# A transformer layer on one core: what the start of attention holds, and where its exponentials are kept

## The chip, the cores and the metric

The kernel runs on one core of a Trainium2 chip, with one launch. The metric is device time in microseconds (us) of that core. A core has a matrix engine (TensorE, "PE" in the profile, its weight loads "PEld"), a vector engine (VectorE, "DVE"), a scalar engine (ScalarE, "ACT"), GpSimd ("POOL") and a sync engine ("SP") that issues DMA transfers. Each runs its own list of instructions in order, and they wait for one another through semaphores. Data lives in SBUF (128 partitions) and in PSUM, eight banks of 128 x 512 f32 that the matmuls write.

## The reference

```python
def _A_ref(x, wqkv, wo):
    ...                                   # H = 32 heads of Dh = 32
    scores = jnp.einsum("bhqd,bhkd->bhqk", q, k) * scale
    p = _softmax(scores, axis=-1)
    o = jnp.einsum("bhqk,bhkd->bhqd", p, v)
    return (lambda x, *d: x.transpose(*d))(o, 0, 2, 1, 3).reshape(B, S, D) @ wo

def _B_ref(x, w1, b1, w2, b2):
    h = jnp.einsum("bsd,df->bsf", x, w1) + b1
    h = _gelu(h)
    return jnp.einsum("bsf,fd->bsd", h, w2) + b2

x = A_x
h = x + _A_ref(_layernorm(x, axis=-1), A_wqkv, A_wo)
h2 = h + _B_ref(_layernorm(h, axis=-1), B_w1, B_b1, B_w2, B_b2)
```

One sequence of 2048 rows, width 1024, FFN width 3584, in bf16. Nothing is masked, so every row attends to all 2048.

## The kernel before

**Tiling.** The rows are 16 tiles of 128, and eight *units* of 256 query rows (`UNITS`). The 32 heads are eight *head groups* g of four heads. A *job* (unit, g) is the attention of one unit in one head group; it has eight *rounds*, each over two key tiles, that is a chunk of 256 keys. A round is:

- a score product on PE (`Att.qk`, L787): eight matmuls into two *score units*. A score unit u is the pair of PSUM banks 2u and 2u + 1. `att.n_units` says how many there are to go round.
- two exponentials on ACT (L797), 128 x 1024 each, from the two score units into a slot of `PT`, a ring of `NR` = 8 slots.
- PV on PE (`Job.pv`, L840): eight matmuls with V into the job's PSUM bank. The denominators stand beside it in the same bank: DVE adds the halves of a slot into `PS` (L855; for units 0 and 1 it also adds two such sums, L861), and PE multiplies the sums by ones (`Job.den`, L878). Some rounds are *direct*: PE takes the exponentials themselves, eight matmuls in place of four, and DVE does nothing.
- at the end of a job `Job.finish` divides (L895 to L909) and writes a 256-wide part of `OT`, from which `wo` later makes the output projection.

PV of a round is added one or two rounds behind its score product.

**Stages.** First the *lead*. Tiles of x land in `xrb`, DVE normalises them (`layer_norm`, L588 to L607) into `xb`, PE transposes them (L613), ACT or DVE copies the result into `xnT` (L620, L622). From it PE makes Q, K and V (`proj_half` and `proj_v1` for head group 0, in chunks of two tiles; `proj` and `proj_v` for the others). In the lead, K of one chunk after the other is made for head group 0, and with each chunk hc the rounds hc of jobs (0, 0) and (1, 0) run. The score units are 0 and 1 (`att.n_units = 2`, banks 0 to 3), banks 4 and 7 serve everything else (`lead_slot`), and 5 and 6 belong to the two jobs.

After the lead the score units are 0, 1 and 2 (banks 0 to 5), and banks 6 and 7 serve all the rest (`slot`). The next jobs are those of

```python
ORDER = [(2, 0)] + [(k, g) for g in range(1, G) for k in range(2)]
```

with the projections of head group g made ahead of its jobs. Then follow units 2 to 7, each beside the FFN of units before it: `wo` (output projection, residual), `ln2`, `ffn1`, `gelu` (its tanh on ACT, L1041), `ffn2`. Queries of units 2 and up go through `q_scratch` in DRAM, made either by `proj` or, from a copy of `xnT` in `x_scratch`, by `late_q`. After the last attention job comes the *tail*: the rest of `wo`, `ln2`, `ffn1` and `ffn2` for unit 7.

`KT` and `V` hold K and V of all head groups for the whole attention. In the lead only head group 0 is in use, and `xb` lies in the area of V of groups 6 and 7.

**Order.** Nothing of the order is written by hand for each engine. Every operation is a task of a graph, with a cost (`occ`), a latency, a priority and what it reads and writes. `Graph.schedule` runs the tasks through a model of the engines, and the order in which they start there becomes each engine's order of instructions. For PE, `pick_pe` chooses: a score product first, then PV when enough rounds wait, then everything else ("bg"). The costs are those of `c_dve`, `c_act`, `MM` and so on; they are in the plan alone.

`OT` is [P, 3, G, 256]: unit qb uses part qb % 3.

Of the kernel before, what the change touches and what calls it, by code (L numbers as in the profile page):

```python
# [12 lines left out]
P = 128  # L13
# [315 lines left out]
def build_kernel(nc, A_x, A_wqkv, A_wo, B_w1, B_b1, B_w2, B_b2, out):  # L329
# [79 lines left out]
    pt_hi = top.cur  # L409
    NS = 3  # L410
    PS, B_PS = sb(top, "PS", [P, NS, 4, 256], BF, NS)
    ot_lo = Area(top.cur)
    OT, B_OT_ = sb(top, "OT", [P, 3, G, 256], BF, 3 * G, 2)
    B_OT = [B_OT_[G * i:G * i + G] for i in range(3)]
# [57 lines left out]
    B_psO = {6: B_ps[6], 5: B_ps[5]}  # L472
    B_psD = {6: gr.buf(), 5: gr.buf()}
# [9 lines left out]
    MM = 0.2195  # L483
    def c_dve_ps(n):
        return (120 + n) / 960.0 + 0.02

    def c_dve(n, x=1):
        return (62 + n / x) / 960.0 + 0.02

    def c_tt(n):  # L490
        return n / 1920.0 + 0.155

    def c_ts(n):
        return n / 3840.0 + 0.165
# [3 lines left out]
    def c_act(n, ap_bias=False):  # L498
        return 0.073 + (0.093 if ap_bias else 0.0) + n / 1200.0

    def pe(fns, occ, reads=(), writes=(), kind="bg", mode="full", prio=0, after=()):
        return gr.add(E.PE, fns, occ, 0.16, reads, writes, prio, kind, mode, after)
# [3 lines left out]

    lead_slots = []

    def lead_slot():
        s = Slot(gr.buf(), 1, (4, 7))  # L510
        s.buf.over.append(B_ps[4])
        B_ps[4].over.append(s.buf)
        lead_slots.append(s)
        return s
# [16 lines left out]
    def mm(bank, lhsT, rhs, start, stop, reads, narrow, cols=(0, 512), after=()):  # L531

        c0, c1 = cols
        occ = MM * (c1 - c0) / 512.0 + 0.003
# [14 lines left out]
    def act(fn, n, reads=(), writes=(), prio=0, ap_bias=False, kind="", after=()):  # L549
        return gr.add(E.Activation, fn, c_act(n, ap_bias), 0.14, reads, writes, prio, kind, after=after)  # L550

    def dve(fn, occ, reads=(), writes=(), prio=0):
        return gr.add(E.DVE, fn, occ, 0.08, reads, writes, prio)
# [25 lines left out]
    def layer_norm(tiles, prio, norm="dve", quick=False):  # L579
# [6 lines left out]
        for k, (x_ap, B_x, o_ap, B_o) in enumerate(tiles):  # L586
            for c in range(2):
                dve(lambda v, c=c, k=k, x_ap=x_ap: v.bn_stats(st_l[:, i + k, 6 * c:6 * c + 6], x_ap[:, 512 * c:512 * c + 512]),  # L588
                    0.68, reads=B_x if isinstance(B_x, list) else [B_x], writes=[B_stl[i + k]], prio=prio)
            dve(lambda v, k=k: v.bn_aggr(mv_l[:, i + k, :], st_l[:, i + k, :]), 0.2,  # L590
                reads=[B_stl[i + k]], writes=[B_mv[i + k]], prio=prio)
        sl = slice(i, i + n)
        if quick:
            dve(lambda v: v.tensor_copy(mvb[:, sl, :], mv_l[:, sl, :]), 0.17, reads=B_mv[sl], writes=B_mvb[sl], prio=prio)
            dve(lambda v: v.tensor_scalar(tb[:, sl, :], mvb[:, sl, 1:2], EPS_BF, None, ALU.add), 0.17,
# [5 lines left out]
        dve(lambda v: v.tensor_copy(mvr[:, sl, :], mvb[:, sl, 0:1]), 0.17, reads=B_mvb[sl], writes=B_mvr[sl], prio=prio)  # L601
        pool(lambda g: g.tensor_tensor(denb[:, sl, 0], tb[:, sl, 0], cexp[:, 0:n], ALU.pow), 0.42 + 0.157 * n,
             reads=B_tb[sl] + [B_cexp], writes=B_denb[sl], prio=prio)
        dve(lambda v: v.reciprocal(rden[:, sl, 0], denb[:, sl, 0]), 0.19, reads=B_denb[sl], writes=B_rden[sl], prio=prio)
        for k, (x_ap, B_x, o_ap, B_o) in enumerate(tiles):
            eng, cost = (dve, 0.58) if norm == "dve" else (pool, 3.8)
# [4 lines left out]
    def transposes(src_ap, B_src, bank, dst_ap, B_dst, evac, prio):  # L611
        for dc in range(DC):
            t = pe(lambda p, dc=dc: p.transpose(psb[:, bi(bank), dc * P:(dc + 1) * P], src_ap[:, dc * P:(dc + 1) * P], ident[:]),  # L613
                   0.064, reads=[B_src, B_ident], writes=[bb(bank)], prio=prio)
# [6 lines left out]
        else:  # L621
            t = dve(lambda v: v.tensor_copy(dst_ap, src()), 0.70, reads=[bb(bank)], writes=[B_dst])  # L622
# [17 lines left out]
    def ln_tiles(tts, prio, norm):  # L640
        layer_norm([x_slot(tt) + (xb[:, tt % NXB, :], B_xb[tt % NXB]) for tt in tts], prio, norm)

    def tr_tile(tt, bank, evac, prio=0):
        tc, t4 = divmod(tt, 4)
        transposes(xb[:, tt % NXB, :], B_xb[tt % NXB], bank, xnT[:, tc, :, t4 * P:(t4 + 1) * P], B_xnTt[tc][t4], evac, prio)

    def proj(which, g, tc, bank, evac, direct=False):
# [7 lines left out]
        elif direct:  # L655
            n = q_slot(0, g, 2)
            q_slots[1, g] = n + 1
# [23 lines left out]
    def load_q(qb, g):  # L681
        if qb < 2:
# [48 lines left out]
    def proj_v1(tt, g, n, bank, evac):  # L731

        for k in range(n):
            tc, t4 = divmod(tt + k, 4)
            for dc in range(DC):
# [5 lines left out]
                reads=[bb(bank)], writes=wr)  # L741
        drop(t, bank)

    def proj_half(which, hc, bank, evac):
# [13 lines left out]
        else:  # L758
            t = dve(lambda v: v.tensor_copy(dst, psum[:, bi(bank), 0:256]), c_dve_ps(256), reads=[bb(bank)], writes=wr)
# [3 lines left out]
    class Att:  # L763
# [8 lines left out]
        def qk(self, job, r):  # L772
# [575 lines left out]
```

## Time and profile before

| | us |
|---|---|
| median of 3 runs | 1092.72 (1091.21 to 1094.55) |
| the profiled execution | 1093.21 |
| its span | 1091.4 |
| PE busy | 1047.8 |
| ACT busy | 1019.5 |
| DVE busy | 789.4 |
| 1024 exponentials (L797) on ACT | 954.0 |
| 12 copies of transposed rows (L620) on ACT in the lead | 11.9 |
| 49 tanhs (L1041) on ACT | 57.9 |

The mean granted TensorE clock was 0.997 of full speed. In the profile's lines "idle before" is the time in which the engine had nothing running ahead of an instruction, and the name behind the arrow is what ended it. Matmuls overlap one another, and the profile models their ends, so a matmul's mean time is longer than the spacing of a row of them; busy PE time is the union of these, and a PE that is busy all the time isn't at its peak. ACT's busy time is a union too: an exponential is listed with a mean of 1168 ns, and 1024 of them cover 954.0 us.

### The profile page before, as it was taken

The numbers are of one execution on the slowest core, as the hardware profiler recorded it, in microseconds if no ns is written. First come the engines' busy times: TensorE is split into PE (matmuls) and PEld (weight loads), VectorE is DVE, ScalarE is ACT, GpSimd is POOL, SyncE is SP. The second block draws the span as 40 slices with busy tenths as digits, with TensorE's granted clock in tenths as the row PEclk, the third lists the DMA queues.
The fourth block names the chain that finished last, engine by engine and source line by source line (L and its number), as shares of the span: only waits on it lengthen the run. The fifth ranks groups of instructions, "written<-read, shape, count | busy, mean of one in ns | idle before, by whom it ended". The sixth has DMA issues, their size and how long they took to land.

```text
span 1091.4 us, 41529 instructions
## 1 busy us (share of the span) xinstructions
PE 1047.8 (96%) x18880; PEld 610.0 (56%) x18930; DVE 789.4 (72%) x1518; ACT 1019.5 (93%) x1124; POOL 28.2 (3%) x78
## 2 busy tenths in 40 slices
PE   7999999998999999999999999999999999999998
PEld 5655555553457446644565466447545754664483
DVE  7657777777778958886589669857885877786511
ACT  4889999999999999999999999999999999999750
POOL 2100000000000000000000000000000000000000
PEclk9999999999899999999999999999999999999999
DMA  7920120035366547555665486467566655975740
GB/s 190 250 83 2 41 83 5 2 133 181 118 186 181 165 154 238 166 174 183 219 176 158 151 249 183 139 193 224 147 199 201 182 173 153 330 225 178 236 156 20
DMA packets 266224, 175.44 MB, mean 161 GB/s; under 512 B 26944, under 2 KB 260416, under 8 KB 265664
## 3 DMA queue, kind: packets, MB, share of 16 engines
q1 hardware_dynamic: 266048, 172.79, 52.0%
q8 instruction: 148, 2.42, 0.9%
q14 instruction: 28, 0.23, 0.1%
HBM read 162.27 MB, written 10.49 MB: 158 GB/s over the span
## 4 chain that ended last, share of the span: by engine, by line
ACT 75%; PE 23%; DVE 1%; issue 1%; DMA 0%; SPq 0%
ACT PT L797 71%; PE ps L541 6%; PE ps L544 5%; PE ps L538 5%; ACT tg L1041 3%; PE ps L787 3%; PE ps L840 2%; PE ps L878 1%; ACT xnT L620 1%; DMA xrb<-in_A_x_dram 0%; PE ps L613 0%; SPq L563 0%; DVE gT L1018 0%; DVE xnT L622 0%; DVE st L588 0%
## 5 line engine op out<-in xcount | busy, mean ns | idle before, releaser
L797 ACT ACTIVATE PT<-ps 128x1024 bf16<-128x1024 f32 x1024 | 954.0, 1168 | 15.9 <-PE ps L787 15.8
L855 DVE TENSOR_TENSOR PS<-PT 128x1024 bf16<-128x1024 bf16 x432 | 288.5, 687 | 121.5 <-ACT PT L797 60.4
L787 PE MATMUL ps<-QT,KT 32*128 32x256 bf16 x4096 | 204.2, 273 | 11.6 <-ACT PT L797 8.1
L840 PE MATMUL ps<-PT,V 128*32 128x256 bf16 x4096 | 176.9, 273 | 2.1 <-ACT PT L797 1.3
L787 PEld LDWEIGHTS ps<-QT,KT 32*128 32x128 bf16 x4096 | 60.9, 92 | 174.0 <-ACT PT L797 162.4
L840 PEld LDWEIGHTS ps<-PT,V 128*32 128x32 bf16 x4096 | 105.0, 97 | 30.8 <-issue 8.3
L541 PE MATMUL ps<-hnT,a_w1r 128*128 128x256 bf16 x906 | 111.5, 273 | 0.7 <-DVE rr L906 0.3
L541 PE MATMUL ps<-a_w2r,gT 128*128 128x512 bf16 x430 | 106.6, 380 | 4.4 <-issue 1.6
L878 PE MATMUL ps<-PS,ones 128*32 128x256 bf16 x1560 | 109.7, 274 | 1.1 <-DVE PS L855 0.5
L538 PE MATMUL ps<-hnT,a_w1r 128*32 128x256 bf16 x2648 | 96.2, 274 | 7.3 <-DVE gT L1018 2.4
L541 PEld LDWEIGHTS ps<-hnT,a_w1r 128*128 128x128 bf16 x906 | 82.8, 98 | 24.8 <-issue 14.5
L538 PE MATMUL ps<-a_w2r,gT 128*32 128x512 bf16 x1304 | 96.5, 381 | 0.1
L1018 DVE TENSOR_TENSOR gT<-ps,b1f 128x512 bf16<-128x512 f32 x98 | 67.3, 687 | 25.5 <-PE ps L538 15.7
L538 PEld LDWEIGHTS ps<-hnT,a_w1r 128*32 128x32 bf16 x2648 | 65.3, 96 | 24.2 <-issue 18.1
L541 PEld LDWEIGHTS ps<-a_w2r,gT 128*128 128x128 bf16 x458 | 39.7, 98 | 52.6 <-issue 12.6
L1041 ACT ACTIVATE tg<-tg 128x1024 bf16<-128x1024 bf16 x49 | 57.9, 1185 | 0.0
L541 PE MATMUL ps<-xnT,Wall 128*128 128x512 bf16 (+1 forms) x238 | 52.2, 354 | 3.4 <-issue 1.3
L878 PEld LDWEIGHTS ps<-PS,ones 128*32 128x32 bf16 x1560 | 41.9, 96 | 17.5 <-issue 5.7
L541 PE MATMUL ps<-a_w1r,OT 128*128 128x512 bf16 x191 | 49.4, 393 | 0.0
L538 PEld LDWEIGHTS ps<-a_w2r,gT 128*32 128x32 bf16 x1304 | 29.2, 96 | 23.1 <-issue 15.0
L895 DVE STREAM_TRANSPOSE OD<-ps 128x256 f32<-128x256 f32 x64 | 28.6, 446 | 12.8 <-PE ps L878 6.5
L1070 DVE SCALAR_TENSOR_TENSOR b_ost<-ps,hch 128x512 bf16<-128x512 f32 x4 | 2.8, 692 | 45.3 <-PE ps L544 45.3
(92 smaller groups left out, 995.1 us busy)
## 6 DMA issues: line engine op xcount, KB each, us to landing
a_w2r<-in_B_w_dram SPq DMA_DIRECT2D x105, 512.0 KB, 5.5
a_w1r<-in_B_w_dram SPq DMA_DIRECT2D x98, 512.0 KB, 4.4
a_w1r<-in_A_wo_dram SPq DMA_DIRECT2D x32, 512.0 KB, 4.2
b_w1r<-in_B_w_dram SPq DMA_DIRECT2D x14, 512.0 KB, 5.3
a_w1r<-in_A_wqkv_dram SPq DMA_DIRECT2D x11, 512.0 KB, 4.5
xrb<-in_A_x_dram SPq DMA_DIRECT2D x16, 256.0 KB, 4.3
Wall<-in_A_wqkv_dram SPq DMA_DIRECT2D x16, 256.0 KB, 4.3
a_w2r<-x_scratch SPq DMA_DIRECT2D x8, 512.0 KB, 4.5
```

Source lines behind the costliest of these rows:

```text
L538: fns.append(lambda p, j=j: p.matmul(psum[32 * j:32 * j + 32, bi(bank), c0:c1], lhsT[:, 32 * j:32 * j + 32], rhs, start=start, stop=stop, ...
L541: t.whole = lambda p: p.matmul(psum[:, bi(bank), c0:c1], lhsT, rhs, start=start, stop=stop, skip_group_check=True)
L544: t = pe(lambda p: p.matmul(psum[:, bi(bank), c0:c1], lhsT, rhs, start=start, stop=stop), occ, reads=reads, writes=[bb(bank)], mode="full" ...
L620: t = act(lambda a: a.activation(dst_ap, src(), ACT.Copy), 1024, reads=[bb(bank)], writes=[B_dst], prio=-1)
L787: return p.matmul(psum[:, 2 * us[h // 2] + h % 2, n * i:n * i + n], KT[32 * h:32 * h + 32, g, k0:k0 + P], QT[32 * h:32 * h + 32, qs, 0:n], ...
L797: act(lambda a, u=u, k=k: a.activation(PT[:, s, k, :, :], psum[:, 2 * u:2 * u + 2, :], ACT.Exp, bias=0.0, scale=SCALE), 1024, reads=[B_ps[ ...
L840: fns.append(lambda p, i=i, h=h: p.matmul(psum[32 * h:32 * h + 32, bi(bank), 0:nq], V[:, g, nk * r + i, 32 * h:32 * h + 32], PT[:, s, h // ...
L855: dve(lambda v: v.tensor_tensor(PS[:, n, :, :], pairs[:, :, 0:256], pairs[:, :, 256:512], ALU.add), c_dve(1024, 2), reads=[B_PT[2 * s], B_ ...
L878: fns.append(lambda p, h=h, rhs=rhs, i=i: p.matmul(psum[32 * h:32 * h + 32, bi(bank), nq:2 * nq], ones32[:, :], rhs, start=False, stop=las ...
L895: t = dve(lambda v: v.transpose(dd, psum[:, bi(bank), nq:2 * nq]), c_dve_ps(nq), reads=[self.B_O, self.B_D], writes=B_D, prio=-1)
L1018: drop(dve(lambda v: v.tensor_tensor(gT[:, fc:fc + 2, cs], psum[:, bi(bank), 0:2 * n].rearrange("p (f c) -> p f c", f=2), b1f[:, fc:fc + 2 ...
L1041: act(lambda a: a.activation(t, t, ACT.Tanh, bias=0.0, scale=math.sqrt(2.0 / math.pi)), c, reads=B_t, writes=B_t, prio=-1)
```

## The change

- The lead has no PV. Its score products go round three score units, banks 0 to 5, and banks 6 and 7 serve the rest, as in the stages behind it. `lead_slot`, `B_psO` and `B_psD` go.
- The exponentials of job (0, 0) fill the eight slots of `PT`. Those of job (1, 0) go into eight new slots `PX`, laid over the areas of K of head groups 2 to 7 and of V of 4 and 5. PV of both jobs comes after all products of V, in two jobs one after the other. Their denominators are made as those of other jobs (sums on DVE) and no longer direct throughout.
- Job (3, 0) joins (2, 0) behind the lead. Q of units 2 and 3 for head group 0 is made in the lead and goes straight into `QT`.
- `OT` has the same size, but a unit uses part u % 2, and a separate part holds (2, 0) and (3, 0).
- The first two tiles are normalised one by one, with the quick form (its small steps on DVE). In the lead ten copies of transposed rows are ACT's (`LEAD_ACT`) and six DVE's, before twelve and four.
- The order of the first loads, priorities in the lead, the number of matmuls that only warm PE up (50, before 56) and most costs and latencies of the planner are others.
- Queries of units 2 and 3 for head group 1 are made after all of `ORDER`, not with head group 3.

```diff
@@ -407,11 +407,26 @@
+    PX, B_PX = [], []
+    for k in range(8):
+        lo = att_lo + 2 * S * (k + 2 if k < 6 else G + k - 2)
+        h_, b_ = sb(Area(lo), "PX%d" % k, [P, 2, 2, 512], BF, 2)
+        PX.append(h_)
+        B_PX += b_
+    B_PT = B_PT + B_PX
+
+    def pt(s):
+        return PT[:, s, :, :, :] if s < NR else PX[s - NR][:, :, :, :]
+
...
-    OT, B_OT_ = sb(top, "OT", [P, 3, G, 256], BF, 3 * G, 2)
-    B_OT = [B_OT_[G * i:G * i + G] for i in range(3)]
+    NOT = 3 * G
+    OT, B_OT = sb(top, "OT", [P, NOT, 256], BF, NOT, 2)
+
+    def ot(u, g):
+        return 2 * G + u if g == 0 and u in (2, 3) else u % 2 * G + g
...
-    MM = 0.2195
+    MM = 0.2133
...
     def c_act(n, ap_bias=False):
-        return 0.073 + (0.093 if ap_bias else 0.0) + n / 1200.0
+        return 0.0615 + (0.093 if ap_bias else 0.0) + n / 1200.0
...
-        occ = MM * (c1 - c0) / 512.0 + 0.003
+        occ = MM * (c1 - c0) / 512.0 + 0.0025
...
+    N_WARM = 50
+    LEAD_ACT = [0, 1, 2, 3, 4, 6, 8, 10, 12, 14]
...
-        def qk(self, job, r):
+        def qk(self, job, r, s=None):
...
-            s = self.rounds % NR
-            self.rounds += 1
+            if s is None:
+                s = self.rounds % NR
+                self.rounds += 1
...
-            if r >= self.nr - self.direct or (self.g == 0 and self.qb < 2):
+            if r >= self.nr - self.direct:
...
     x_tile(0, -6)
-    x_tile(1, -6)
     load_w(WQ, -5, 0, P)
+    x_tile(1, -5)
     load_w(WK, -5, 0, P)
     x_tile(2, -5)
     x_tile(3, -5)
-    load_w(WV, -5, 0, 256)
     for tt in range(4, 8):
         x_tile(tt, -5)
+    load_w(WV, -5, 0, 256)
...
-    att.n_units = 2
...
+    ORDER = [(2, 0), (3, 0)] + [(k, g) for g in range(1, G) for k in range(2)]
+    made = []
     last_x = []
+    lead = []
     lead_norm(0)
     for hc in range(8):
         ev = "act" if hc == 0 else "dve"
         if hc < 2:
-            proj_half(0, hc, lead_slot(), ev)
-        proj_half(1, hc, lead_slot(), ev)
+            proj_half(0, hc, slot(), ev)
+        proj_half(1, hc, slot(), ev)
         if hc < 7:
             lead_norm(hc + 1)
-        proj_v1(2 * hc, 0, 2, lead_slot(), ev)
         for k, r in {0: [(0, 0)], 1: [(0, 1), (1, 0), (1, 1)]}.get(hc, [(0, hc), (1, hc)]):
-            s = att.qk((k, 0), r)
-            pending.append((lead_jobs[k], r, s))
-            attention_drain(LEAD_LAG)
-    attention_drain()
-    att.n_units = 3
-    att.unit = 0
-    N_LEAD = sum(t.kind == "pv" for t in gr.tasks)
...
+            lead.append((k, r, att.qk((k, 0), r, NR + r if k else None)))
+    if ORDER[0] == (2, 0):
+        proj(0, 0, 1, slot(), "dve", direct=True)
+        made.append(0)
+    for hc in range(8):
+        proj_v1(2 * hc, 0, 2, slot(), "dve")
+    pv_last += [t for t in gr.tasks if t.eng == E.PE and t.kind == "bg"]
+    for k in range(2):
+        job = Job(k, 0, slot(2))
+        for k_, r, s in lead:
+            if k_ == k:
+                job.pv(r, s)
+    N_LEAD = 0
+    pool_banks = {6: [], 7: []}
     lx = last_x[-1:]
...
-            if g == 3 and EARLY:
-                for g_ in range(2):
-                    if g_ not in made:
-                        made.append(g_)
-                        proj(0, g_, 1, slot(), "dve")
```

## The prediction

> **What bounds the kernel now.** I read the page's head and its chain first, then busy time by stage.
>
> ```profile
> span 1091.4 us, 41529 instructions
> ...
> ACT 75%; PE 23%; DVE 1%; issue 1%; DMA 0%; SPq 0%
> ```
>
> ACT carries the chain. A table of stages (columns: stretch, length, then busy us of PE, PEld, DVE, ACT and POOL with instruction counts, granted TensorE clock, DMA share, GB/s) cuts the span where ACT changes character: its first copy of normalised rows at 10.68, the start of the long unbroken row of exponentials at 65.66, the end of the last exponential near 1028.5.
>
> ```profile
> 10.68:65.66 54.98, 48.65 (x911) 32.17 (x912) 37.96 (x97) 42.58 (x47) 8.20 (x21) 1.00 0.76 210
> 65.66:1028.50 962.84, 932.16 (x17469) 533.36 (x17507) 733.58 (x1381) 956.84 (x1041) 15.61 (x42) 1.00 0.52 160
> 1028.50:1091.40 62.90, 59.40 (x454) 38.45 (x456) 11.98 (x28) 18.84 (x36) 1.54 (x2) 1.00 0.36 121
> ```
>
> In the middle ACT idles 962.84 - 956.84 = 6.0 us: it is the bound. In the lead it idles 54.98 - 42.58 = 12.4 us. In the tail PE is the bound. So the time is lead + ACT's middle + tail. The timeline shows what the lead loses:
>
> ```profile
> 46.84 0.40 PE L787 MATMUL ps<-QT,KT 32*128 32x256 bf16 x8
> ...
> 47.29 1.94 ACT L797 ACTIVATE PT<-ps 128x1024 bf16<-128x1024 f32 x2 [0.51 <-PE ps L787]
> ...
> 49.28 0.40 PE L787 MATMUL ps<-QT,KT 32*128 32x256 bf16 x8
> ```
>
> A score round takes two score units; the lead has only two, so each round starts after the exponentials of the one before, and ACT waits 0.5 us for it: 2.44 us a round (46.84 to 49.28). In the middle, 225 exponentials took 206.38 us in the chain: 0.917 each, 1.83 a round.
>
> **The lead.** Three units remove that wait. What can set the pace then is ACT itself, or the key chunks that DVE delivers. I walked the new order of instructions with durations from the old timeline. First exponentials: tile 0 is now normalised alone, but tile 1 lands one 256 KB weight transfer later and both are needed for the first Q and K; I get about 15.2 instead of 16.17. The wide value weights now come after x tiles 4 to 7, and ten value products stand ahead of the first score round. The bytes up to them are 3.07 MB; 171 GB/s over the first 5 us and 316 over the next 5 put them near 12, two us before PE gets there (price if late: us for us). Second round: it needs DVE's copies of Q and K of the second chunk, behind 12 statistics and six normalisations as before; about 22.4, against 22.84. From there ACT owes 15 rounds, 30 x 0.917 = 27.5 us, and five copies of rows (tiles 6, 8, 10, 12, 14), 5 x 0.92 = 4.6: end at 54.5 if it never waits. DVE, up to the eighth key copy, holds 32 statistics (20.8 us in the old groups), 16 normalisations (8.1), 16 aggregates (3.0), some 22 small ones (3.5), six copies of rows at 0.69, seven key, one query and three value copies at 0.42, one wide copy (0.69) and, new there, six sums at 0.69: 49 us of group times, of which 10% overlaps (the groups of the first 50 us add up to 42.4, the stretches to 38.1): 44 us. From 3.52, fully busy after 1.5 us of waits, that is 49.2; at the 86% that DVE reached from 20 to 45 us, 54.9. Add a score round (0.4) and the last two rounds of exponentials (3.7): 53.3 to 59.0. I take 56.0, between ACT's 54.5 and DVE's worse end. The 17th round started at 65.66, and ACT's debt behind it is the same: **-9.7 us** (-6.7 at 59.0; -12.7 if the second round comes 1.5 us sooner than I walked and ACT never waits).
>
> PV, its denominators and most of V leave the lead; its matmul time through the 16th round falls by 10.5 us, and that work goes behind. Two copies of rows move from ACT to DVE (2 x 0.92, counted above). Unit 2 and 3's queries for head group 0 go straight to QT, so one store and two reloads leave SP's queue, 0.32 us of issue each, hidden.
>
> **The middle.** Exponentials and tanhs are the same, so its length changes only with ACT's idle time. Counting columns in both orders at 0.216 us per 512 (28 such took 6.05 us in the tail, from 1069.77 to 1075.82), PE owes 803 us between the 16th and the last score round before and 816 after: +13, although denominators of pair sums save 2.3. The cover is PE's own idle time, 962.8 - 932.2 = 30.7. That it can be used is shown by
>
> ```profile
> 630.00:660.00 30.00, 29.91 (x611) 20.16 (x603) 22.85 (x43) 30.00 (x34) 0.00 (x0) 1.00 0.81 246
> ```
>
> PE at 99.7% beside an ACT that never waits. The planner's cost of a 512-column product falls from 0.2225 to 0.2158, the spacing measured, so it packs more between two rounds and keeps less to spare. I put +1.2 us for places where that is too much (bounds 0 and all 13, nearer to nothing because of this row). DVE gets 20 more sums, 14 us against 229 us idle here: nothing.
>
> The middle has a second price. In the old run PE had no filler while the last job of unit 1 closed:
>
> ```profile
> 266.00:268.00 2.00, 1.16 (x32) 0.34 (x20) 0.91 (x2) 2.00 (x3) 0.00 (x0) 1.00 0.98 290
> ...
> 270.00:272.00 2.00, 1.24 (x28) 0.56 (x28) 0.17 (x2) 2.00 (x4) 0.00 (x0) 1.00 1.05 361
> 272.00:274.00 2.00, 0.44 (x8) 0.12 (x8) 1.97 (x6) 2.00 (x4) 0.00 (x0) 0.61 0.09 30
> 274.00:276.00 2.00, 1.96 (x12) 0.72 (x13) 1.25 (x3) 2.00 (x3) 0.00 (x0) 0.50 0.11 33
> 276.00:278.00 2.00, 2.00 (x13) 0.44 (x10) 1.05 (x2) 0.73 (x1) 0.00 (x0) 0.50 0.03 8
> 278.00:280.00 2.00, 2.00 (x14) 0.63 (x6) 0.69 (x1) 1.65 (x2) 0.00 (x0) 0.68 0.00 0
> ```
>
> After six us at some 60% and one at 22% the granted clock fell to 0.50 for about 6.9 us, and ACT waited 2.7 us for score rounds. In the new order that hole is two rounds long instead of five, but a new one appears late: rounds 463 to 467 of 512 have attention products alone, since PE has caught up and waits for the layer norm of unit 6. The first dip stays with a chance of 0.7, the second comes with 0.8: 1.5 dips for one, +1.3 (bounds -2.7, +2.7). Middle together **+2.5**.
>
> **The tail.** Behind the last score round the old order has 31 products of the second FFN matrix as filler, the new one 5: 26 x 0.216 = 5.6 us less PE work. It lay beside the chain that leads to the last layer norm:
>
> ```profile
> 1031.05 1.04 PE L544 MATMUL ps<-a_w1r,OT 128*128 128x512 bf16 x4
> ...
> 1031.92 5.13 PE L541 MATMUL ps<-a_w2r,gT 128*128 128x512 bf16 x22
> ...
> 1035.87 0.55 DVE L607 TENSOR_SCALAR b_xb<-hch,mvr,rden 128x1024 bf16<-128x1024 bf16 x1
> ...
> 1036.89 0.61 PE L613 MATMUL ps<-ident,b_xb 128*128 128x128 bf16 x8
> ```
>
> The transposes follow the normalised rows, not the filler, so nothing is won. But PE now stands idle some 4 us there, just before 50 us in which it is the bound. If the clock falls as at 272, PE starts those at half rate; with 3.4 to 6.9 us of it, 1.7 to 3.4 us are lost. I take **+1.8** (bounds 0, 3.4).
>
> [...]
>
> **Sum.** 1093.21 (the profiled execution: 1091.4 span and 1.8 around it) - 9.7 + 2.5 + 1.8 = 1087.8. That execution lay 0.5 above the median, so 1087.3; I say **1087**.
>
> **Rivals.**
> - *DVE sets the lead.* Sums and two more copies stand in its queue ahead of the last key copies. For it: 86% in the old lead with fewer of them. Against: its old waits were for PE's products of keys, values and queries (4.4, 2.5 and 1.2 us), and PE has less ahead of these now. At 59.0 for the 17th round: 1087.3 + 3.0 = 1090.3.
> - *PE's debt comes back.* The 13 us find no cover, ACT waits. For it: the chain of waits runs through PE in several long stretches (304 to 336, 416 to 451). Against: the window above, and fewer products behind the last round in the new order. Half of it: 1092.6.
> - *Slower: the clock falls in the lead itself.* For it: without PV, PE has 26 us of columns in the 41 us from the first score round to the 17th (64%), against 36 in 48 (75%) before, and only some 58% until the second round. Against: the old lead had PE busy 66% from 15 to 20 us and kept clock 1.00; the stretch at 266 had 59% before it fell. Each dip costs 2.7 us, and 41 us hold at most four. Two undo the gain, from the third on it is slower; four: 1087.3 + 10.8 = 1098.1.
> - *The change doesn't do what it says:* exponentials kept in K and V areas hold up the key copies of later head groups, or the join of 2 and 3 only shifts work. Against: in the new order all PV of the lead stands before the first product of head group 1. Time: as before, 1092.7.
>
> **How the numbers follow.** About 0.3% is what a measurement of this kernel can tell from no change: 1089.4 to 1096.0 is "same". Forecast 0.70 (its own range 1080 to 1090.5, 0.06 of it above 1089.4); DVE 0.12 (half of it short of 59.0 and below 1089.4); debt 0.05 (0.02 of it at the full price, slower); clock 0.08, slower; nothing gained 0.05 (0.02 of it slower). Faster: 0.64 + 0.06 = 0.70. Slower: 0.02 + 0.08 + 0.02 = 0.12. Same: 0.18. The range's low end is the lead's good bound with neither the middle's nor the tail's price (1087.3 - 3.0 - 2.5 - 1.8 = 1080); its high end, 1094, takes in the DVE case, half the debt and no gain, and leaves out some 0.15.
>
> **What would show it.** Right: score rounds about 1.9 us apart in the lead and ACT without gaps from about 22 us; the 17th round near 56; ACT idle in the middle between 4 and 12 us; a clock of 0.5 near the last sixth of the span and again right after the last exponential. Wrong: key copies late on DVE (17th round at 59 or later); clock under 1.00 before 60 us; many gaps of 0.2 us in ACT's row, which would be the debt.

## The result: slower by half a per cent

The changed kernel takes 1098.3 us (median of 5 runs, 1097.01 to 1100.16), the kernel before 1092.72 beside it: a ratio of 1.0055, 95% interval 1.0038 to 1.0072. The forecast was 1087, faster. The profiled execution of the changed kernel took 1099.77.

From its page, the head and the chain of work that ended last:

```profile
span 1098.0 us, 40837 instructions
...
PE 64%; ACT 29%; DVE 4%; issue 1%; DMA 1%; SPq 0%; DVEq 0%
```

Before, ACT had 75% of this chain. Now PE has most of it: work that used to lie beside ACT now sets when ACT may go on. The table by stage (columns as in the prediction's: stretch, length, busy us of PE, PEld, DVE, ACT, POOL, clock, DMA share, GB/s), cut where the 17th score round's exponentials start and where the last exponential ends:

```profile
10.00:54.58 44.58, 37.49 (x557) 26.67 (x559) 40.53 (x105) 38.89 (x45) 8.36 (x21) 1.00 0.83 217
54.58:1033.75 979.17, 951.52 (x17534) 540.55 (x17527) 737.33 (x1401) 963.00 (x1042) 19.34 (x42) 0.99 0.52 159
1033.75:1098.00 64.25, 55.77 (x433) 37.33 (x431) 11.27 (x27) 18.97 (x36) 1.54 (x2) 0.97 0.28 92
```

| | before | changed | difference | forecast |
|---|---|---|---|---|
| lead, to the 17th round's exponentials | 65.66 | 54.58 | -11.1 | -9.7 |
| middle | 962.8 | 979.2 | +16.4 | +2.5 |
| tail | 62.96 | 64.25 | +1.3 | +1.8 |
| span | 1091.4 | 1098.0 | +6.6 | -5.4 |

Lead and tail came as forecast; the middle took the whole gain back and more. In the timeline of the lead (start, length, instruction) the score rounds now stand 1.81 us apart (44.84 to 46.65), where they stood 2.44 apart, and from 24 us to the 17th round the view of waits names none of ACT's:

```profile
44.84 0.40 PE L794 MATMUL ps<-QT,KT 32*128 32x256 bf16 x8
45.41 2.09 ACT L805 ACTIVATE PX<-ps 128x1024 bf16<-128x1024 f32 x2
...
46.65 0.40 PE L794 MATMUL ps<-QT,KT 32*128 32x256 bf16 x8
```

In the middle ACT idles 979.17 - 963.00 = 16.2 us, before 6.0. The view of waits, cut to the middle (who waits for whom: us in total, times, longest):

```profile
ACT PT L805 <- PE ps L794: 14.1, 14, 2.2
ACT PT L805 <- PE ps L849: 1.5, 1, 1.5
```

These are few and long waits, not the many of 0.2 us that I had named as the sign of PE's debt. ACT's busy time rose too, by 6.1 us (963.00 against 956.84) for the same 992 exponentials and 49 tanhs; the one instruction more in the table is an exponential that the edge of the stretch cuts. The groups of instructions (name, shape and count, then busy us and mean ns of one, then idle time before them) give a hint how; of the changed kernel, from its 17th round to 1017 us:

```profile
L805 ACT ACTIVATE PT<-ps 128x1024 bf16<-128x1024 f32 x974 | 905.3, 1059 | 16.2 <-PE ps L794 14.1 <-PE ps L849 1.5
```

and of the kernel before, from its own 17th round to 1017 us:

```profile
L797 ACT ACTIVATE PT<-ps 128x1024 bf16<-128x1024 f32 x980 | 911.4, 1173 | 6.7 <-PE ps L787 6.5
```

An exponential that lists 1173 ns but costs 0.92 in a row overlaps its neighbour, so its scores lay ready. I read the mean of 1059 as a sign that many scores came only just in time in the changed kernel. The busy time of these rows doesn't show the rise by itself: it is 0.93 us an exponential in both.

### The profile page after: what moved, and what is told of

It reads as the page before. It is cut to its first block, busy times and chain, and to the rows that moved or that the text cites. A ratio compares the mean times of both kernels' runs of the same rounds, so it can differ in the third digit from the quotient of the medians.

```text
span 1098.0 us, 40837 instructions
## 1 busy us (share of the span) xinstructions
PE 1051.3 (96%) x18559; PEld 609.6 (56%) x18559; DVE 794.4 (72%) x1546; ACT 1022.7 (93%) x1122; POOL 32.1 (3%) x77
## 3 DMA queue, kind: packets, MB, share of 16 engines
q8 instruction: 145, 2.38, 0.9%
## 4 chain that ended last, share of the span: by engine, by line
PE 64%; ACT 29%; DVE 4%; issue 1%; DMA 1%; SPq 0%; DVEq 0%
ACT PT L805 27%; PE ps L545 24%; PE ps L542 13%; PE ps L794 10%; PE ps L849 7%; PE ps L548 5%; PE ps L889 4%; DVE PS L866 1%; PE ps L617 1%; ACT PX L805 1%; ACT xnT L624 1%; ACT tg L1050 1%; DMA xrb<-in_A_x_dram 0%; DMA a_w1r<-in_A_wo_dram 0%; DVE st L592 0%
## 5 line engine op out<-in xcount | busy, mean ns | idle before, releaser
L805 ACT ACTIVATE PT<-ps 128x1024 bf16<-128x1024 f32 x1008 | 938.4, 1060 | 18.8 <-PE ps L794 16.7
L545 PE MATMUL ps<-hnT,a_w1r 128*128 128x256 bf16 x1044 | 130.8, 277 | 0.5 <-issue 0.4
L545 PEld LDWEIGHTS ps<-hnT,a_w1r 128*128 128x128 bf16 x1044 | 96.9, 99 | 29.5 <-issue 16.7
L542 PE MATMUL ps<-a_w2r,gT 128*32 128x512 bf16 x1416 | 101.6, 381 | 0.4 <-DVE gT L1052 0.2
L542 PE MATMUL ps<-hnT,a_w1r 128*32 128x256 bf16 x2096 | 77.7, 274 | 7.9 <-issue 4.4
L542 PEld LDWEIGHTS ps<-hnT,a_w1r 128*32 128x32 bf16 x2096 | 51.4, 96 | 23.4 <-issue 17.4
L1050 ACT ACTIVATE tg<-tg 128x1024 bf16<-128x1024 bf16 x49 | 51.9, 1068 | 0.0
L545 PE MATMUL ps<-xnT,Wall 128*128 128x512 bf16 (+1 forms) x226 | 46.5, 343 | 2.4 <-ACT xnT L624 1.8
L542 PE MATMUL ps<-xnT,Wall 128*32 128x512 bf16 x600 | 42.0, 381 | 0.2 <-DVE V L734 0.2
L1079 DVE SCALAR_TENSOR_TENSOR a_ost<-ps,hch 128x512 bf16<-128x512 f32 x28 | 19.1, 683 | 27.3 <-PE ps L542 22.2
```

Of the source, the lines that this page charges most:

```text
L542: fns.append(lambda p, j=j: p.matmul(psum[32 * j:32 * j + 32, bi(bank), c0:c1], lhsT[:, 32 * j:32 * j + 32], rhs, start=start, stop=stop, ...
L545: t.whole = lambda p: p.matmul(psum[:, bi(bank), c0:c1], lhsT, rhs, start=start, stop=stop, skip_group_check=True)
L805: act(lambda a, u=u, k=k: a.activation(pt(s)[:, k, :, :], psum[:, 2 * u:2 * u + 2, :], ACT.Exp, bias=0.0, scale=SCALE), 1024, reads=[B_ps[ ...
L1050: act(lambda a: a.activation(t, t, ACT.Tanh, bias=0.0, scale=math.sqrt(2.0 / math.pi)), c, reads=B_t, writes=B_t, prio=-1)
L1079: drop(dve(lambda v, o=o, hs=hs, bank=bank: v.scalar_tensor_tensor(R.ost[o][:, :], psum[:, bi(bank), :], 0.5 if half else 1.0, hch[:, hs, ...
```

## The experiments

The texts written before the runs number their theories by batch. In the first four, theory 1 is PE's debt (the work that left the lead finds no room beside ACT), theory 2 the planner's new, lower costs alone, theory 3 the join of (3, 0). In the next four, theory 1 is that the new costs pack PE so full that it owes more than ACT leaves room for. In the four with moved lists, theory 2 is that PE waits for blocks of instructions. In the following table the stages are of each run's profiled execution; "stalls" is the sum of PE's idle times of at least 0.5 us behind the 17th round that wait for nothing the profile shows ("issue"); "left" is how many products of the second FFN matrix the order leaves behind the last score round. Ratios are to the kernel before, run beside it.

| run | median us | ratio, 95% interval | 17th round | middle | tail | stalls | left |
|---|---|---|---|---|---|---|---|
| before | 1092.72 | | 65.66 | 962.8 | 62.96 | 1.2 | 87 |
| changed | 1098.3 | 1.0055 (1.0038 to 1.0072) | 54.58 | 979.2 | 64.25 | 8.3 | 61 |
| a_oldcost | 1100.85 | 1.0074 (1.0048 to 1.0099) | 65.96 | 963.8 | 70.42 | 5.1 | 123 |
| b_newcost | 1107.87 | 1.0128 (1.0104 to 1.0152) | 66.52 | 975.5 | 64.03 | 5.3 | 56 |
| a_pecost | 1102.14 | 1.0084 (1.0067 to 1.0102) | 54.98 | 964.3 | 81.90 | 5.4 | 164 |
| a_no30 | 1103.42 | 1.0096 (1.0072 to 1.0120) | 62.86 | 977.0 | 64.24 | 7.8 | |
| a_mixcost | 1093.57 | 1.0004 (0.9986 to 1.0023) | 54.73 | 970.3 | 70.39 | 6.4 | 123 |
| a_oldcost_warm | 1111.85 | 1.0164 (1.0142 to 1.0186) | 60.55 | 968.6 | 79.26 | 4.5 | 181 |
| a_less | 1098.93 | 1.0045 (1.0031 to 1.0058) | 54.41 | 976.9 | 64.11 | 6.5 | |
| b_less | 1105.6 | 1.0126 (1.0098 to 1.0155) | 65.69 | 974.3 | 64.17 | 4.2 | |
| b_shift64 | 1095.45 | 1.0006 (0.9992 to 1.0019) | 66.68 | 964.6 | 63.00 | 3.3 | 87 |
| b_shift128 | 1098.55 | 1.0040 (1.0024 to 1.0057) | 66.87 | 964.5 | 63.06 | 4.7 | 87 |
| a_shift64 | 1099.24 | 1.0050 (1.0032 to 1.0067) | 56.41 | 980.7 | 64.67 | 8.8 | 61 |
| a_shift128 | 1097.29 | 1.0023 (1.0008 to 1.0039) | 54.98 | 977.8 | 65.47 | 8.0 | 61 |
| a_tailfill | 1096.24 | 1.0023 (1.0008 to 1.0038) | 55.86 | 975.2 | 62.96 | 6.7 | 61 |
| a_mix2155 | 1089.34 | 0.9960 (0.9945 to 0.9975) | 54.20 | 966.5 | 64.70 | 2.5 | 75 |
| a_mix2180 | 1086.68 | 0.9928 (0.9905 to 0.9951) | 54.23 | 963.2 | 65.28 | 3.0 | 98 |
| a_mix2180_s64 | 1084.49 | 0.9902 (0.9883 to 0.9921) | 54.54 | 962.8 | 65.14 | 5.0 | 98 |
| a_mix2180_s128 | 1083.68 | 0.9891 (0.9867 to 0.9914) | 56.57 | 962.1 | 65.13 | 3.9 | 98 |
| b_2180 | 1094.15 | 0.9993 (0.9979 to 1.0007) | 65.23 | 965.3 | 62.39 | 3.1 | 86 |

### Structure or costs

The changed kernel with every cost of the planner as before (a_oldcost), the kernel before with every new cost (b_newcost), the changed kernel with only PE's costs as before (a_pecost), and the changed kernel with (3, 0) not joined (a_no30):

```diff
-    MM = 0.2133
+    MM = 0.2195
...
-        return 0.0615 + (0.093 if ap_bias else 0.0) + n / 1200.0
+        return 0.073 + (0.093 if ap_bias else 0.0) + n / 1200.0
...
-        return gr.add(E.DVE, fn, occ, 0.135, reads, writes, prio)
+        return gr.add(E.DVE, fn, occ, 0.08, reads, writes, prio)
```

> The changed kernel with all of the planner's costs and latencies as before the change; the structure (lead without PV, three score units, PX, join of (3, 0)) stays. Theory 1, PE's debt: PE has hardly any time to spare, so the PV and V work that left the lead must be paid somewhere. In the order of this kernel PE owes 807 us of columns between the 16th and the last score round, as before the change (805), and the rest stands behind the last round (68.1 us against 60.5 before the change and 55.0 in the changed kernel). So: 17th round near 54.6, middle 963 to 966 us with ACT idle 6 to 9, tail 62.9 + 7.6 = 70.5, time about 1091 (1089 to 1093). Theory 2, the tight costs alone did the harm: middle 963, tail 63, time 1082 to 1084.

> The kernel before with the new costs and latencies of the planner, nothing else. In its order PE owes 813 us of columns in the middle (805 before) and 53.1 behind the last score round (60.5). Theory 1, PE's debt: about 1093 to 1096, since lead and PE's total are as before and the 7 us only move from the tail, where some of them were hidden, into the middle. Theory 2, the tight costs did the harm: 1098 or more, with ACT idle over 14 us in the middle.

> The changed kernel with PE's costs alone as before the change (DVE's, ACT's and all latencies stay new). Its order leaves 794 us of columns to the middle and 79.1 behind the last round. Theory 1, PE's debt: ACT is saturated in the middle (about 958 to 962 us, idle under 5), and 79.1 - 60.5 = 18.6 us are added to the tail's 62.9: 54.6 + 960 + 81.5 + 1.8 = 1098 (1095 to 1100). Theory 2: 1084 to 1088.

> The changed kernel without the join of (3, 0): (2, 0) alone follows the lead, its Q through DRAM as before the change. Its order has 820 us of columns in the middle and 52.7 behind the last round. If the join did the harm (theory 3): 1090 to 1094. If it is PE's debt (theory 1): 1097 to 1101, PE's work is the same and head group 1 must be ready 14.7 us sooner.

The new costs lengthen the middle, on either structure. With old costs the changed kernel's middle is 963.8, 1.0 over the kernel before; with new costs the middle of the kernel before is 975.5, 12.7 over. With new costs except PE's it is 964.3, but 164 products stay behind and the tail is 81.9: PE does less in the middle, and the time, 1102.14, is no better than the changed kernel's. The join is no cause: without it the middle is 977.0, and a_no30 is late by its lead (62.86).

Whole times say less than stages here. Old costs don't make the changed kernel faster (1100.85), since they cost it 11.4 us in the lead and 6.2 in the tail; none of the four runs is as fast as the kernel before.

a_oldcost missed its expected time in the lead alone, which shows the rival "the clock falls in the lead itself". Its table of stretches (the last three columns are clock, DMA share, GB/s):

```profile
32.00:38.00 6.00, 3.47 (x32) 1.85 (x32) 4.38 (x12) 4.32 (x5) 1.12 (x3) 0.66 1.07 254
38.00:44.00 6.00, 4.71 (x40) 2.71 (x32) 4.63 (x12) 4.72 (x5) 1.13 (x3) 0.50 1.12 271
44.00:51.00 7.00, 6.48 (x58) 4.71 (x58) 4.41 (x11) 5.33 (x6) 1.56 (x3) 0.50 1.01 251
```

PE was busy 58% from 32 to 38 us; the clock fell to 0.50 at 33.9 and stayed there until 51.0, though PE was busy 79 and 93% in the next two stretches. What 0.50 costs stands in the changed kernel's trace: 13 products of 256 columns took 2.95 us at 0.50 (from 326.76 us) and 1.59 at 1.00 (from 330.19). Shorter falls, of 3.4 us, came in the leads of a_no30, a_shift64, a_tailfill and a_mix2180_s128 too, not in the profiled execution of the changed kernel. That is five of the 14 traces with this lead, and none of the six with the old one: this lead, without PV, carries the risk.

### The amount of work, and the lead's costs alone

a_mixcost plans the lead with the new costs and all behind it with the old ones (a flag `C` is switched once the lead's tasks are made). a_oldcost_warm is a_oldcost with useless matmuls in the lead. a_less and b_less leave work out in both kernels:

```diff
+    C = [True]
...
-        occ = MM * (c1 - c0) / 512.0 + 0.0025
+        occ = (MM if C[0] else MMO) * (c1 - c0) / 512.0 + (0.0025 if C[0] else 0.003)
...
+        pe([lambda p, bank=bank: p.matmul(psum[:, bi(bank), 256:512], ident[:, :], b2t[:, 0:256], start=True, stop=True)] * 6, 0.66,
+           reads=[B_ident, B_b2t], writes=[bb(bank)])
...
-                    for dc in range(DC):
+                    nd = DC - 1 if 1 <= u <= 5 else DC
+                    for dc in range(nd):
```

> The changed kernel; the planner uses the new costs while it plans the lead and the old, looser costs behind it. Theory 1 (the tight costs pack PE fuller than ACT can bear, and what they pull forward is paid as ACT's waits; with loose costs the same work is paid behind the last score round): 17th round near 54.6 if the clock stays at 1.00 in the lead, middle near 964 with ACT idle 6 to 9 us, tail near 70.4 (123 products of the second FFN matrix behind the last score round, as in the run with all costs old), together 1089 +/- 2. Rival (the middle of the changed order is long whatever the costs, since PV of the lead is owed in it): middle 972 or more, time 1097 or more.

> The changed kernel with all costs as before, and 60 useless matmuls of 256 columns (6 us) in the lead, six behind each half of a Q or K product of head group 0, so that PE has fewer holes there. If the clock fell to half in the lead of the run with old costs because PE was too empty: no dip before 60 us, 17th round at 55 to 57 in place of 65.96. If the dip has another cause: 17th round still at 64 or later. The order leaves 77.1 us of matmul columns behind the last score round (68.1 without the useless ones), so tail 78 to 80; middle 958 to 964; 1092 to 1099 in all by the first, 1100 or more by the second.

> The changed kernel with one of eight products in each group of the first FFN matrix of units 1 to 5 left out: some 15 us less work on PE, nothing less on ACT. Theory 1 (PE's debt fills the middle): the middle falls from 979 to 963 to 967, ACT idles 3 to 7 us in place of 16, tail 62 to 64, time 1080 to 1084. Rival (ACT's waits come from the order of the work or from falls of the clock, not from its amount): middle 974 or more, time 1092 or more.

> The kernel before with the same products left out as in the changed kernel's run of this batch (one of eight in each group of the first FFN matrix of units 1 to 5). ACT has only 6 us of idle time in its middle, so theory 1 gives a middle of 958 to 962 and a tail of 55 to 63: 1083 to 1090, and the changed kernel with the same left out is 5 to 9 us faster than this one, where it is 5.6 us slower with all the work. Rival: the changed kernel stays slower than or equal to this one without those products too.

Theory 1 fell in the form in which I held it. With 15 us of products less (5 units, 28 products of 256 columns each, 0.108 us apiece) the changed kernel is no faster (middle 976.9, where 963 to 967 was expected), and the kernel before even 1.3% slower. That the changed kernel is now the faster of the two agrees with one of the expected numbers, but not with its reason: both middles are long. Less work on PE doesn't bring the middle back. But the test isn't clean, since less filler makes more thin places, and in b_less the clock fell: PE was 67% busy from 905 to 910 us and the clock 1.00, and from 910 to 915 it was 0.50,

```profile
905.00:910.00 5.00, 3.34 (x81) 1.59 (x80) 2.54 (x4) 5.00 (x7) 0.00 (x0) 1.00 1.06 370
910.00:915.00 5.00, 3.52 (x46) 1.14 (x43) 2.66 (x7) 5.00 (x6) 0.00 (x0) 0.50 0.10 33
```

and again near 780, 937, 1035 and 1047. Of the 9.8 us by which ACT idles more in b_less's middle than in that of the kernel before (15.8 and 6.0), 5.0 are waits at the lowered clock (6.9 and 1.9); its order differs elsewhere too, and the rest stays open.

a_oldcost_warm had no fall before 60 us, and its 17th round came at 60.55 in place of 65.96: the emptiness of PE was a cause, but 55 to 57 was expected, so it was not the only one (the useless matmuls themselves stand in PE's way). In the whole they cost more than they brought (1111.85). a_mixcost is level with the kernel before: its lead keeps 10.9 us, and the tail gives 7.4 back. Its profiled execution, 3.7 us above the median, gives back another 7.5 in the middle: 970.3, where 964 was expected and 972 or more by the rival. Its runs spread widely, from 1088.88 to 1101.63, and 6.4 of ACT's 11.8 idle us in this middle stand right behind stalls of the following kind.

### Stalls that wait for nothing

In the changed kernel's view of waits of PE, over the middle:

```profile
PE ps L542 <- issue: 4.6, 4, 2.3
PE ps L849 <- issue: 2.8, 3, 1.2
PE ps L794 <- issue: 1.4, 1, 1.4
```

One of them cuts a score product in two (timeline of PE):

```profile
659.11 0.28 PE L794 MATMUL ps<-QT,KT 32*128 32x256 bf16 x1
660.74 0.39 PE L794 MATMUL ps<-QT,KT 32*128 32x256 bf16 x7 [1.35 <-issue]
```

The eight matmuls are one task of the plan, and the trace names nothing that the second of them waits for. And the longest starts a chain of its own: PE stands 2.29 us, ACT gets its scores 2.23 us late, the clock is 0.50 from 326.71 for 3.41 us, and at 330.31 ACT has waited another 1.49 us.

```profile
325.55 0.95 PE L542 MATMUL ps<-hnT,a_w1r 128*32 128x256 bf16 x28 [2.29 <-issue]
...
326.88 1.94 ACT L805 ACTIVATE PT<-ps 128x1024 bf16<-128x1024 f32 x2 [2.23 <-PE ps L794]
330.31 3.79 ACT L805 ACTIVATE PT<-ps 128x1024 bf16<-128x1024 f32 x4 [1.49 <-PE ps L794]
```

The page's list of DMA queues has one for instructions:

```profile
q8 instruction: 145, 2.38, 0.9%
```

2.38 MB in 145 packets are 16.4 KB each, and the 37118 matmuls and loads of this trace are 255.98 to a packet (before: 37810 and 148 packets, 255.5). So I counted PE's matmuls and weight loads up to each stall of at least 0.5 us, modulo 256. In the changed kernel:

| stall ends at, us | us | matmuls and loads so far | modulo 256 |
|---|---|---|---|
| 60.21 | 0.52 | 1467 | 187 |
| 325.55 | 2.29 | 10911 | 159 |
| 547.94 | 1.23 | 19321 | 121 |
| 660.74 | 1.35 | 23397 | 101 |
| 741.80 | 1.14 | 26199 | 87 |
| 839.86 | 1.78 | 29509 | 69 |

The remainder falls steadily, as it would if stalls came every 256th instruction of PE's list and the list also held a few that the count misses. In the other runs they lie on such lines too, all but three of 98. This gave theory 2: PE waits for its next block of instructions, a packet of that queue. The trace's own list of packets has the times: the six stalls end 1.34 to 1.54 us after a packet of this queue has landed, and 96 of the 98 stalls of all twenty runs do so 1.2 to 1.6 us after one. At the ends of the six stalls 5, 42, 75, 91, 102 and 115 packets had landed: from the first to the last, 110 packets to 28042 matmuls and loads, 254.9 each (between the two stalls of the kernel before, 31 and 7886, 254.4). With 145 packets in the span, six stalls cost 0.5 us or more, up to 2.29 us.

To test theory 2, the useless matmuls at the very start were cut in smaller pieces, so that all that follows stands 64 or 128 places further back in the same order:

```diff
-        pe(lambda p: p.matmul(psum[:, 4, 0:256], ident[:, :], b2t[:, 0:256], start=True, stop=True), 0.153,
+        m = 1 + 32 * (k + 1) // 50 - 32 * k // 50
+        c = 256 // m // 32 * 32
+        pe([lambda p, c=c: p.matmul(psum[:, 4, 0:c], ident[:, :], b2t[:, 0:c], start=True, stop=True) for j in range(m)], 0.153,
```

> The kernel before, with 32 of its 56 useless matmuls at the start cut in two halves of 128 columns: the same work in the same order, but every later PE instruction stands 64 places further back. In every run so far PE's stalls over 0.5 us that wait for nothing the profile shows fall on one line, instruction number modulo 256 (187 early to 69 late in the changed kernel). Theory 2 (PE stands until its next block of 256 instructions is there, 16 KB over the DMA engines, late when these are full; where the blocks end is chance, and the kernel before has only two such stalls, 1.2 us in all, against six of 8.3 in the changed one and 4.2 to 7.8 in the other runs): the stalls move to other instructions, all on that line again, with 3 to 8 us in all, and the time rises to 1095 to 1101. Theory 1 (only the fullness of the plan counts): time 1092 to 1094, as before.

> As the run with 64 places, with 128 places. Theory 2: other instructions again, 3 to 8 us of such stalls, 1095 to 1101. Theory 1: 1092 to 1094.

> The changed kernel with the same cut: its later PE instructions stand 64 places further back, in the same order. Theory 2: the stall of 2.29 us at 325 us and the fall of the clock right behind it are gone or elsewhere; stalls of 3 to 8 us in all, on the same line modulo 256 but at other instructions; time anywhere from 1090 to 1100, and not tied to 1098.3. Theory 1: 1097 to 1100, ACT's idle places where they were (326.9, 549, 661, 744, 841 us).

> As the changed kernel's run with 64 places, with 128 places. Theory 2: stalls at other instructions, 1090 to 1100. Theory 1: 1097 to 1100, ACT's idle places where they were.

The stalls stayed on the line and moved to other instructions: the changed kernel's 19321 (remainder 121) is a stall again with 64 places more, at an instruction 64 places earlier in the program; 2.29 us at 325 is gone in both, and the fall of the clock behind it. With the packets' landings, that speaks for blocks of about 256, as theory 2 has them. The time moved less than expected: the kernel before became slower by 0.06% (not to be told from none) and 0.40%, the changed kernel stayed between 1.0023 and 1.0055. Places of block ends are worth some 0.3%, and the kernel before had good luck (1.2 us of stalls against 3.3 and 4.7). But at all three places the changed kernel's middle is long: 979.2, 980.7 and 977.8 against 962.8, 964.6 and 964.5. Chance is not the cause.

The stalls themselves carry a large part of the loss, though. This is ACT's idle time in the middle and, of it, its waits that end within 3 us behind a stall's end (one to a stall):

| list moved by | before: idle, behind stalls | changed | a_mix2180 (below) |
|---|---|---|---|
| 0 | 6.0, 0.9 | 16.2, 8.8 | 5.8, 2.8 |
| 64 | 7.3, 3.1 | 17.3, 7.9 | 5.4, 4.8 |
| 128 | 7.5, 3.1 | 14.8, 8.5 | 5.4, 4.5 |

On the mean of the three places ACT idles 9.2 us more in the changed kernel, and 6.0 of these stand behind late blocks. Why its plan meets more of them, wherever the blocks end, isn't shown. That the blocks come late because the DMA engines are full is likely, since the DMA share in the changed kernel's stalls and the 6 us ahead of each was 0.70 to 1.07 against 0.52 over the middle, but it was not tried.

### The price of a product, and the tail

Back to the costs, with the lead kept. a_mix2180 and a_mix2155 are a_mixcost with a 512-column product behind the lead at 0.221 and 0.2185 (old 0.2225); a_tailfill is the changed kernel with useless products in the hole ahead of the last layer norm; b_2180 is the kernel before at 0.221; the two others are a_mix2180 with its PE list moved by 64 and 128 places.

```diff
-    MMO = 0.2195
+    MMO = 0.2180
...
+            for k in range(15):
+                d = mm(fb, ident[:, :], b2t[:, 0:512], True, True, [B_ident, B_b2t], False, after=[end])
```

> The changed kernel with new costs for the lead's plan and old ones behind it, but a 512-column product behind the lead at 0.221 (old 0.2225, new 0.2158). The order leaves 98 products of the second FFN matrix behind the last score round (123 with the old price, 61 in the changed kernel, 87 before). If a middle price trades between ACT's waits and the tail: 17th round near 54.6, middle 965 to 970, tail 64.5 to 66, time 1088 to 1092, faster than before by 1 to 5 us. If the waits come back as soon as the price falls: middle 973 or more, 1095 or more.

> The same with a product at 0.2185; 75 products of the second FFN matrix are left behind the last score round. Trade theory: middle 970 to 976, tail 63 to 65 (a short fall of the clock in it), time 1090 to 1096, slower than the run at 0.221. If only the sum of PE's work counted, the two runs would agree within 2 us.

> The changed kernel with 15 useless products of 512 columns (3.2 us) behind unit 7's output projection, where PE stood idle ahead of the last layer norm. If the clock falls there because PE is empty: no clock under 1.00 behind the last exponential, tail 62.5 to 63.2 in place of 64.25 to 65.5, and the middle as in the changed kernel (977 to 981); 1096 to 1099 in all. If the clock falls for another reason: dip and tail stay.

> The same with 64 places: 1084 to 1091 if the gain isn't luck, 1092 or more if it is.

> The run with a product at 0.221 behind the lead, and 64 more useless matmuls at the start (the old ones cut smaller), so that all later PE instructions stand 128 places further back. If its gain over the kernel before is the change's and the plan's, it stays faster: 1084 to 1091, 17th round near 54.6, middle 961 to 968. If it was a lucky place of PE's block ends, it comes back to 1092 or more, with stalls of 5 us or more in place of 3.0.

> The kernel before with only the price of a 512-column product lowered in the same way (0.2225 to 0.221). If the gain of the run with that price came from the price alone, this is as fast, 1084 to 1090. If it needs the changed lead: 17th round near 65.7 as before, 1090 to 1097.

a_mix2180 is faster than the kernel before by 0.72% (0.49 to 0.95), and so than the changed one too; with its list moved the gain is 0.98 and 1.09%, so it isn't luck. The price alone does nothing that can be told to the kernel before (0.9993). All of a_mix2180's difference from the changed kernel lies in the costs behind the lead. Its stages and its chain:

```profile
10.00:54.23 44.23, 37.25 (x555) 26.40 (x556) 40.19 (x103) 38.61 (x45) 8.33 (x21) 1.00 0.86 229
54.23:1017.42 963.19, 942.54 (x17462) 535.67 (x17454) 743.03 (x1400) 957.42 (x1042) 16.90 (x42) 1.00 0.53 160
1017.42:1082.70 65.28, 61.82 (x469) 39.52 (x467) 12.17 (x28) 19.04 (x37) 1.53 (x2) 0.99 0.35 117
```

```profile
ACT 74%; PE 22%; DMA 2%; DVE 1%; issue 1%; SPq 0%; DVEq 0%
```

ACT is the bound again and idles 5.8 us in the middle, as before; PE holds 942.5 us there, 10.4 more than before: what left the lead found its cover. The tail is 2.3 us longer, the lead 11.4 shorter, and the sum, with 0.4 of the middle, is the -8.7 between the two spans.

a_mix2155 costs 2.7 us more, in the direction of the trade, though the intervals of the two ratios overlap, and its middle of 966.5 is shorter than the 970 to 976 expected. But it also bounds the trade: its plan takes 8.48 products to a round (two exponentials of 0.9263 over 0.2185), and so does the changed kernel's (0.9148 over 0.2158), and its trace has 815.5 us of columns between the 16th and the last round (at 0.216 us per 512), against 818.2. One middle is 966.5, the other 979.2. So most of the changed kernel's loss isn't in the price of a product against an exponential; it is in the other new costs and latencies, together with it. Of the 9.9 us by which ACT idles more in the changed kernel's middle (16.2 against 6.3), 6.0 are waits behind late blocks (8.8 against 2.8). Which of the costs it is stays open: they weren't tried one by one, and a_pecost, which keeps the new ones except PE's, has a short middle only together with the longest tail.

In a_tailfill the clock stayed at 1.00 behind the last exponential. The hole in the changed kernel, in the timeline and the table of stretches:

```profile
1042.18 0.62 PE L617 MATMUL ps<-ident,b_xb 128*128 128x128 bf16 x8 [4.07 <-DVE b_xb L611]
```

```profile
1042.00:1044.00 2.00, 0.71 (x10) 0.54 (x11) 1.90 (x7) 1.02 (x1) 0.56 (x1) 0.88 1.09 348
1044.00:1046.00 2.00, 2.00 (x20) 2.00 (x21) 1.42 (x4) 0.00 (x0) 0.43 (x1) 0.50 1.09 358
```

and the corresponding stretch of a_tailfill:

```profile
1043.00:1045.00 2.00, 2.00 (x36) 1.83 (x34) 0.37 (x1) 1.63 (x2) 0.00 (x0) 1.00 1.10 375
```

Its tail is 62.96 in place of 64.25: the 1.3 us are the clock of 0.50 after the hole, 3.41 us of it from 1043.51 in the changed kernel. (Its middle, 975.2, came out shorter than the 977 to 981 expected, with 6.7 us of stalls in place of 8.3.)

## Why the prediction was wrong, by its steps

- **The lead** was right: 54.58 for the 17th round where 56.0 stood, within 53.3 to 59.0. ACT set the pace, not the key copies: 54.5 was the sum for an ACT that never waits. The fall of the clock in the lead did not happen in this kernel's profiled execution, but in those of five of its relatives. That 41 us hold at most four dips was the prediction's estimate, and no run shows it; a_oldcost had one fall, of 17.1 us.
- **The middle** failed, at this step: "I put +1.2 us for places where that is too much (bounds 0 and all 13, nearer to nothing because of this row)". The middle grew by 16.4. I set PE's 13 us of extra columns against its 30.7 us of idle time and took one stretch of 30 us with a full PE as proof that the cover can be used. It can: a_mix2180 uses it. What I priced too low was the plan itself. Changing the planner's costs was to me a detail that fits PE a little fuller; by b_newcost it is 12.7 us on its own, with no debt from any lead. The sum by parts that the runs support: the lead -11.1, the new costs in the middle 12.7 (from b_newcost) to 16 (979.2 against a_mix2180's 963.2), the tail +1.3. In the trace the 16.4 us are 10.2 of more idle and 6.1 of more busy ACT. Of the idle time 8.8 us stand behind six late blocks of instructions, 0.9 behind two before; a term for them is nowhere in my sum. Some 2 us of that is the kernel before's luck (its stalls have a mean of 3.1 us at three places, the changed kernel's of 8.4).
- **"PE's debt comes back"** got a chance of 0.05. In a_oldcost, a_pecost and a_mixcost the debt does come back, behind the last score round (tails of 70.4, 81.9 and 70.4); in the changed kernel the amount of the debt isn't what brings the waits, since a_mix2155 owes 815.5 us of columns in its middle, only 2.7 less, and has one of 966.5.
- **Falls of the clock in the middle** were half right. The late one came where rounds 463 to 468 are thin (931 to 940 us): the clock was low from 937.7 to 944.5 us, and that cost ACT 1.3 us. The one at 272 went entirely; another came at 326, behind a stall of 2.29 us whose place the old profile doesn't foretell. Two in place of one, where the sum had 1.5. Its price was too high: in the old trace ACT's waits at 272 add up to 1.9 us, not 2.7. And the fall there began at 272.4, ahead of the stretch of 22% and of PE's gap of 1.4 us, with PE 58% busy from 266 on (3.75 of 6.44 us).
- **The tail** was right, mechanism and size: a hole of 4.07 us where "some 4" stood, a clock of 0.50 behind it for 3.41 us (from 1043.51), +1.3 where +1.8 stood. With the list moved, the tails of 64.67 and 65.47 are 1.7 and 2.4 us above those of the kernel before.
- The forecast 1087 lies near what a_mix2180's plan gives (1083.7 to 1086.7), but that agreement is partly chance: a_mix2180's terms are -11.4, +0.4 and +2.3, where -9.7, +2.5 and +1.8 stood. It was a forecast for the structure, made for a kernel that changes structure and plan at once.

## What to carry to other kernels

A planner's costs are part of the program: a diff that touches them needs a run of its own, old structure with new costs and new structure with old costs, before any gain or loss is put down to the structure. Here, on the same lead, new costs behind it gave 1.0055 of the time before, old costs 1.0004, and old costs with a 512-column product at 0.221 (old 0.2225, measured spacing 0.216) 0.9928. A stage that got shorter is no gain until the others are read beside it: work that a plan leaves out of the middle stands in the tail (a_pecost: 964.3 and 81.9). And taking work away from an engine can come with a slower kernel: b_less, with 15 us of products less, took 1.0126 of the time before, and 5.0 of the 9.8 us by which ACT idled more in its middle were waits at a clock under 1.00.

## What the hardware showed that I had not expected

- PE stood still now and then for 0.5 to 2.3 us, 1.2 to 8.8 us in all in a span of 1090. 95 of the 98 such stalls lie on lines of the instruction count modulo 256, and 96 ended 1.2 to 1.6 us after a packet of the instruction queue had landed. Moving the list by 64 or 128 places moved the time of the same order by up to 0.4%.
- The clock of PE fell where PE was 58% busy and had no gap over 0.6 us (before, 266 to 272.4 us). In a_oldcost it stayed at 0.50 for 17.1 us (33.9 to 51.0), with PE 79 to 93% busy from 38 us on. Other falls lasted 3.41 us (changed kernel, from 326.71 and from 1043.51) and 6.83 us (before, from 272.44; changed kernel, from 937.70).
- Leaving out 15 us of products made the kernel before 1.3% slower, 1105.6 us in place of 1093.2 beside it.
